# Another scratch layout for the first layer's weights, a bank pair for the first group's second scores, and a new order of the first block

## The chip, the cores and the metric

The kernel runs on one core of a Trainium2 chip. The metric is the device time of one execution in microseconds; the runs shown are three executions of the kernel before, and one more execution was profiled. Everything is in 32-bit floats at the interface.

## The reference

Local attention in chunks of 64 tokens, followed by a two-layer network with a squared ReLU:

```
q, k, v: (8, 8, 576, 64)          # batch, heads, tokens, head size
scores = q_c @ k_c^T / 8          # per head and chunk of 64 tokens
attn = exp(scores - max) / (sum + 1e-9)
x = (attn @ v_c) as (4608, 512)   # tokens x model
h = x @ w_in                      # w_in (512, 2048)
g = s * max(h, 0)^2 + b
out = g @ w_out                   # w_out (2048, 512)
```

## The kernel before

Tokens lie on 36 tiles of 128. Four tiles (512 tokens) are one column block of the first stage, which is called the layer here: two early attention groups of two tiles each, `one` and `two`, make its x, and 16 steps `up` (x times a slice of w_in, L634) and `down` (L609) run over 16 slices of the hidden dimension. The other 32 tiles are four blocks of eight tiles. In them a block of w_in or w_out is multiplied with seven products instead of eight (`p1` to `p7`, L690), with sums of quarters of the weights (units s1 to s4) and of the tokens (t1 to t4) as operands beside the plain quarters 11, 12, 22. The first of these blocks makes the sums of w_in itself (`s_add`, `s_hi`, `s_lo`); its down product is direct. The later three blocks read everything from scratch in DRAM.

Every number in a product is held as a high part and a remainder in the fast 32-bit format (`hi`, then `lo`), and a product is three matmuls: high by high, high by remainder, remainder by high.

The weights arrive as 64-bit words, in 16 pairs of 1 MB (`load0` to `load15`, L157; pair 0 in halves a and b). For each pair ScalarE runs `scale` (L172) and `tail` (L176), VectorE `shift` (L182) and `sign` (L184), GpSimd `add` (L190), ScalarE `hi` (L194) and VectorE `lo` (L198). After `lo`, SyncE stores high part and remainder to scratch: pairs of w_in by `in0` to `in7` (L204), those of w_out by `out0` to `out7` (L219), the sums by `s_keep0` to `s_keep7` (L204). The scratch of w_in is one array in the order in which the later blocks use its 56 units of 256 KB, four to a tile; so a store of a pair is cut into pieces of one or two units, and a later block loads a tile of four units with one DMA. The first block loads the exact units alone, in 14 tiles that hold one to three of them (`ring0` to `ring13`), and keeps the sums in SBUF. The pool `raw` with three buffers holds the words, and later these tiles: a load waits until the third tile before it has been used up. All these DMAs are issued by SyncE, in one queue, in order; one that waits holds up those behind it.

An early group runs in halves i = 0, 1: `scores` (L464), `peak` (L470), `sub` (L476), `exp` (L480), `sum` (L486), `normz` (L490, L491), `norm` (L495), `transposes` (L504), `copies` (L509), `values` (L516), `x_hi` (L524), `x_lo` (L528). Both halves of the scores share one PSUM tile of two banks. `up1a` and `up0a` work on the 256 tokens of `one`, `up1b` and `up0b` on those of `two`. Groups `three` to `six` make the tokens of the first block; their steps are whole (scores L368, peak L373, sub L378, sum L387, transposes L404).

Up to the end of the first block's products the order of the work is written out by hand: the string `ORDER` names the steps, and each engine takes its own in that order. `keep_busyN` is filler on TensorE, N matmuls on a tile of ones, each recorded as two instructions (L126). `s_and_b` (L1104) turns the two scalars s and b into columns with TensorE, and `sb` (L1167) copies them with VectorE. `up` of step j writes one of two PSUM banks in turn; from j = 2 on, `relu`, `square`, `g_hi` (ScalarE) and `g_lo` (VectorE, L655) read that bank, and it is free after `g_lo`. In the first block, tokens' sums are made by `xt1.add_dve` and so on (L561), and split by `.hi` (L565) and `.lo` (L570); `s_add` is four subtractions or additions (L233).

## Time and profile before

| | us |
|---|---|
| median of three runs | 786.3 |
| lowest and highest | 785.7, 787.04 |
| the profiled execution | 786.62 |
| its span from first to last instruction | 784.6 |
| TensorE busy | 771.6 |
| VectorE busy | 616.0 |
| ScalarE busy | 469.9 |
| GpSimd busy | 48.7 |

Times within the span are counted from its start. "Busy" of TensorE is the time in which a matmul is running by the profile; weight loads run beside it. A row of the timeline gives start, duration, engine, source line, operation, tiles and shapes, and in brackets how long the engine had been idle and what ended that. Durations of neighbours overlap a little, so that the distance of two starts is shorter than a duration.

### The profile page before, as it was taken

The numbers are of one execution on the slowest core, as the hardware profiler recorded it, in microseconds if no ns is written. First come the engines' busy times: TensorE is split into PE (matmuls) and PEld (weight loads), VectorE is DVE, ScalarE is ACT, GpSimd is POOL, SyncE is SP. The second block draws the span as 40 slices with busy tenths as digits, with TensorE's granted clock in tenths as the row PEclk, the third lists the DMA queues.
The fourth block names the chain that finished last, engine by engine and source line by source line (L and its number), as shares of the span: only waits on it lengthen the run. The fifth ranks groups of instructions, "written<-read, shape, count | busy, mean of one in ns | idle before, by whom it ended". The sixth has DMA issues, their size and how long they took to land.

```text
span 784.6 us, 13847 instructions
## 1 busy us (share of the span) xinstructions
PE 771.6 (98%) x5572; PEld 638.1 (81%) x5572; DVE 616.0 (79%) x892; ACT 469.9 (60%) x645; POOL 48.7 (6%) x23
## 2 busy tenths in 40 slices
PE   6899999999999999999999999999999999999997
PEld 6787887888888888888888888888888888888886
DVE  5988899998579986888899858888998723348773
ACT  3899877767653433566864635666846346575442
POOL 1453440000000000000000000000000000000000
PEclk9999999999999999999999999999999999999999
DMA  9999998778568999866566587765565778886653
GB/s 360 346 346 340 353 321 294 257 242 264 186 220 292 317 352 325 326 258 229 174 214 215 188 300 290 250 263 204 171 229 178 241 262 294 295 269 215 210 192 135
DMA packets 79988, 204.33 MB, mean 260 GB/s; under 512 B 5812, under 2 KB 39348, under 8 KB 68660
## 3 DMA queue, kind: packets, MB, share of 16 engines
q1 hardware_dynamic: 79488, 203.05, 74.4%
q8 instruction: 44, 0.72, 0.4%
q10 hardware_dynamic: 436, 0.39, 0.1%
q14 instruction: 20, 0.16, 0.1%
HBM read 159.38 MB, written 44.04 MB: 259 GB/s over the span
## 4 chain that ended last, share of the span: by engine, by line
PE 89%; ACT 4%; DVE 3%; DMA 3%; issue 0%; POOL 0%; DVEq 0%; ACTq 0%
PE ps_h L690 22%; PE ps_h L910 17%; PE ps_o L690 17%; PE ps_x L910 8%; PE ps_x L609 7%; PE ps_o L910 4%; PE ps_o L609 4%; PE ps_h L609 3%; PE ps_h L634 3%; PE ps_a L368 2%; DMA raw<-in_w_dram 1%; PE ps_x L424 1%; DMA w_out<-t 1%; ACT t L172 1%; PE ps_a L424 1%; ACT raw L176 1%
## 5 line engine op out<-in xcount | busy, mean ns | idle before, releaser
L690 PE MATMUL ps_h<-t,raw 128*128 128x512 f32 x672 | 167.3, 391 | 0.0
L690 PEld LDWEIGHTS ps_h<-t,raw 128*128 128x128 f32 x672 | 125.4, 188 | 26.5 <-ACT u L700 0.2
L910 PE MATMUL ps_h<-t,raw 128*128 128x512 f32 x576 | 142.0, 389 | 0.0
L884 DVE TENSOR_TENSOR t<-t 128x512 fp32r<-128x512 f32 (+1 forms) x120 | 105.2, 897 | 33.2 <-ACT t L882 33.2
L910 PEld LDWEIGHTS ps_h<-t,raw 128*128 128x128 f32 x576 | 108.0, 188 | 22.5
L690 PE MATMUL ps_o<-t,raw 128*128 128x512 f32 x480 | 121.8, 389 | 0.0
L709 DVE TENSOR_TENSOR t<-ps_o,u 128x512 f32<-128x512 f32 x96 | 66.0, 690 | 67.7 <-PE ps_o L690 62.4
L690 PEld LDWEIGHTS ps_o<-t,raw 128*128 128x128 f32 x480 | 90.1, 188 | 18.8
L700 ACT COPY u<-ps_h 128x512 f32<-128x512 f32 x96 | 56.0, 585 | 69.8 <-PE ps_h L690 68.9
L882 ACT CAST t<-t 128x512 fp32r<-128x512 f32 (+1 forms) x120 | 87.4, 790 | 2.8 <-PE ps_h L910 1.9
L412 DVE STREAM_TRANSPOSE pT<-p 32x256 f32<-32x256 f32 x192 | 83.7, 436 | 3.2
L910 PE MATMUL ps_x<-t,raw 128*128 128x512 f32 x288 | 73.1, 389 | 0.0
L753 ACT ACTIVATE t<-t 128x1024 f32<-128x1024 f32 x64 | 67.2, 1053 | 0.2
L910 PEld LDWEIGHTS ps_x<-t,raw 128*128 128x128 f32 x288 | 54.1, 188 | 11.3
L749 ACT ACTIVATE t<-t 128x512 f32<-128x512 f32 (+1 forms) x64 | 54.1, 846 | 10.3 <-DVE t L709 9.9
L190 POOL TENSOR_TENSOR t<-t,raw 128x1024 int32<-128x1024 int32 (+1 forms) x17 | 48.0, 2821 | 68.3 <-DVE t L184 47.8
L609 PE MATMUL ps_x<-t,raw 128*128 128x512 f32 x192 | 48.9, 390 | 0.0
L634 PE MATMUL ps_h<-x,t 128*128 128x512 f32 (+1 forms) x216 | 47.5, 371 | 1.1 <-DVE x L528 0.7
L914 ACT ACTIVATE u<-ps_h,shift,sb 128x512 f32<-128x512 f32 x18 | 13.1, 779 | 58.2 <-PE ps_h L910 58.2
L634 PEld LDWEIGHTS ps_h<-x,t 128*128 128x128 f32 x216 | 37.0, 188 | 8.5 <-DVE x L528 1.0
L609 PEld LDWEIGHTS ps_x<-t,raw 128*128 128x128 f32 x192 | 36.0, 188 | 7.5
L910 PE MATMUL ps_o<-t,raw 128*128 128x512 f32 x144 | 36.5, 389 | 0.0
(129 smaller groups left out, 1013.7 us busy)
## 6 DMA issues: line engine op xcount, KB each, us to landing
raw<-w_in SPq DMA_DIRECT2D x42, 1024.0 KB, 5.5
raw<-w_out SPq DMA_DIRECT2D x34, 1024.0 KB, 5.3
raw<-w_sum SPq DMA_DIRECT2D x24, 1024.0 KB, 5.0
raw<-in_w_dram SPq DMA_DIRECT2D x15, 1024.0 KB, 7.5
qk<-in_qkv_dram SPq DMA_DIRECT2D x15, 1024.0 KB, 8.4
w_out<-t SPq DMA_DIRECT2D x16, 512.0 KB, 6.8
w_sum<-t SPq DMA_DIRECT2D x16, 512.0 KB, 9.1
v<-in_qkv_dram SPq DMA_DIRECT2D x15, 512.0 KB, 4.7
```

What stands on the lines that cost most here:

```text
L190: nc.gpsimd.tensor_tensor(out=i, in0=i, in1=low.bitcast(I32), op=ALU.add)
L412: nc.vector.transpose(out=self.pT[k].rearrange("p i a t -> p (i a) t")[:, :, t], in_=p[t, :, k])
L609: nc.tensor.matmul(out=self.ps[m], lhsT=x, rhs=y, start=(j == 0 and i == 0), stop=(j == stop and i == 2))
L634: nc.tensor.matmul(out=self.ps[j][:, cols], lhsT=w[:, c, :], rhs=x[:, c, :], start=(c == 0 and i == 0), stop=(c == NHP - 1 and i == 2))
L690: nc.tensor.matmul(out=ps, lhsT=w[:, e, :], rhs=y[:, e, :], start=start and e + i == 0, stop=e + i == 3, skip_group_check=not start)
L700: nc.scalar.copy(out=u, in_=self.a[p])
L709: nc.vector.tensor_tensor(out=self.tile(p, h)[:, e, :], in0=ps, in1=u, op=ALU.add)
L749: nc.scalar.activation(out=t, in_=t, func=AF.Relu)
L753: nc.scalar.activation(out=t, in_=t, func=AF.Square)
L882: nc.scalar.copy(out=hi, in_=f)
L884: nc.vector.tensor_tensor(out=lo, in0=f, in1=hi.bitcast(F32), op=ALU.subtract)
L910: nc.tensor.matmul(out=self.acc[name][m], lhsT=x, rhs=y, start=new and q == 0, stop=q == 2, skip_group_check=not new)
```

## The change

- w_in's scratch becomes nine arrays: one for each of eight quarters of the exact units (`w_in[e]`, two to four units, 11 and 12 of step p beside 22 of step p - 1), and `w_in_sum` with a whole tile of four sums per step. `in` stores 11 and 12 together; `keep` is a single DMA.
- The first block loads its exact units in 8 tiles in place of 14, so the ring has 11 loads in `ORDER` in place of 17. The later blocks still take four units per tile; each load is now cut into as many DMAs as the four units have separate places (three or four).
- Group `one` takes a PSUM tile of its own for the scores of half 1, from the pool of one bank pair that the transposes use.
- `ORDER` is new. The steps are the same but for the filler: `keep_busy` 28 in place of 31, and `warm1.12`, 12 filler matmuls into the bank of `up1`. Steps `bias` and `exps` are defined and not used.

```diff
 ORDER = """
-one.load_qk0 one.load_qk1 three.load_qk load0b load0a two.load_qk0 two.load_qk1 two.load_v one.scores0 one.peak0 one.load_v s_and_b
-sb one.sub0 one.exp0 one.scores1 keep_busy7 load1 one.sum0 one.peak1 three.load_v one.normz0 one.sub1 one.norm0
-one.exp1 four.load_v tail0b one.transposes0 keep_busy3 one.sum1 one.normz1 one.copies0 load2 one.norm1 tail0a scale0a
-one.transposes1 four.load_qk shift0a scale0b two.scores0 keep_busy8 one.copies1 sign0a shift0b add0a two.peak0 two.sub0
...
-two.norm0 two.normz1 two.transposes0 keep_busy2 one.x_hi1 shift1 two.copies0 two.norm1 two.values0 sign1 two.transposes1 two.x_hi0
-one.x_lo1 two.copies1 add1 two.x_lo0 up1a scale2 tail2 two.values1 shift2 up0a hi1 sign2
-two.x_hi1 three.scores lo1 add2 two.x_lo1 in1 three.peak scale3 up1b tail3 three.sub up0b
...
-g_hi3 three.norm down0 scale4 g_lo1 hi3 shift4 relu2 g_lo3 three.transposes sign4 square2
-g_hi2 down1 load6 lo3 tail5 scale5 add4 g_lo2 in2 three.copies up4 shift5
...
+one.load_qk0 one.load_qk1 two.load_qk0 load0b load0a three.load_v one.load_v two.load_qk1 three.load_qk one.scores0 one.peak0 one.scores1
+keep_busy3 s_and_b sb one.sub0 one.peak1 one.exp0 load1 two.scores0 keep_busy13 one.sum0 one.sub1 two.load_v
+tail0b two.peak0 one.exp1 one.normz0 two.sub0 load2 tail0a one.sum1 scale0a one.norm0 two.exp0 four.load_v
+scale0b one.normz1 one.transposes0 keep_busy3 shift0a shift0b one.copies0 four.load_qk one.norm1 one.values0 sign0b one.transposes1
+one.x_hi0 sign0a two.scores1 keep_busy3 one.copies1 add0b two.sum0 one.x_lo0 two.peak1 add0a hi0b one.values1
+keep_busy6 two.sub1 one.x_hi1 lo0b load3 hi0a one.x_lo1 two.exp1 lo0a up1a two.sum1 in0
+two.normz0 tail1 up0a two.norm0 two.normz1 scale1 two.norm1 two.transposes0 shift1 two.copies0 two.transposes1 sign1
+two.values0 two.copies1 three.scores two.x_hi0 add1 tail2 two.x_lo0 two.values1 scale2 three.peak two.x_hi1 shift2
+hi1 three.sub sign2 three.exp two.x_lo1 add2 three.sum warm1.12 up1b tail3 load4 up0b
+scale3 three.normz lo1 relu1 open_o hi2 three.norm in1 up3 square1 relu0 shift3
+g_hi1 lo2 load5 square0 scale4 three.transposes sign3 out0 relu3 g_hi0 up2 shift4
+three.copies add3 square3 tail4 four.scores scale5 g_lo0 load6 g_lo1 hi3 down0 five.load_qk
+four.peak relu2 g_hi3 lo3 square2 tail5 shift5 in2 down1 sign4 g_hi2 sign5
+tail6 scale6 add4 g_lo2 g_lo3 up4 four.sub four.exp add5 load7 hi4 up5
...
+    SUMS = ("s2", "s3", "s1", "s4")
+    quarters = [[(0, "11"), (0, "12")]] + [[(p, "11"), (p, "12"), (p - 1, "22")] for p in range(1, NP)]
+    quarters[-1].append((NP - 1, "22"))
...
-    w_in = scratch.tile([P, 7 * NP // 4, 2, 4, 2 * P], F32, name="w_in")
+    w_in = [scratch.tile([P, 2, len(us), 2 * P], F32, name="w_in%d" % e) for e, us in enumerate(quarters)]
+    w_in_sum = scratch.tile([NP, P, 2, 4, 2 * P], F32, name="w_in_sum")
...
-            keep_units(units[p, "11"], i, even[:, 0:1, :])
-            keep_units(units[p, "12"], i, even[:, 1:2, :])
-            keep_units(units[p, "22"], i, odd[:, 1:2, :])
+            for name, n, source in (("11", 2, even), ("22", 1, odd[:, 1:2, :])):
+                e, u = unit_at[p, name]
+                nc.sync.dma_start(out=w_in[e][:, i, u:u + n, :], in_=source)
...
         def keep(self):
...
+            nc.sync.dma_start(out=w_in_sum[self.p], in_=self.t.bitcast(F32))
...
+                    places = [(w_in_sum[p], SUMS.index(k)) if k in SUMS else (w_in[unit_at[p, k][0]], unit_at[p, k][1])
+                              for p, k in source]
+                    u = 0
+                    while u < 4:
+                        n, (w, at) = u + 1, places[u]
+                        while n < 4 and places[n][0] is w and places[n][1] == at + n - u:
+                            n += 1
+                        nc.sync.dma_start(out=o[:, :, u:n], in_=w[:, :, at:at + n - u])
+                        u = n
...
         def scores(self, i):
-            if i == 0:
-                self.ps = self.banks(0)
+            if i == 0 or self.tb == 0:
+                self.ps[i] = self.banks(i)
+            else:
+                self.ps[i] = self.ps[0]
...
+        def warm(self, j, n):
+
+            for _ in range(n):
+                nc.tensor.matmul(out=self.ps[j][:, 2 * P:3 * P], lhsT=ones, rhs=ones, start=True, stop=True)
```

In the first block the new order of the tokens' sums and of the sums of w_in stands in the same string: before, VectorE's queue ends `... s_add0 lo15 s_add7 s_add5 s_lo0 s_lo1 g_lo15 s_add6 xt1.add_dve x22.lo xt3.add_dve xt1.lo xt2.add_dve xt3.lo seven.peak xt2.lo`; after, `... s_add7 g_lo15 g_lo14 s_lo0 lo15 s_add3 s_add5 s_add2 xt1.add_dve x22.lo xt3.add_dve xt1.lo xt2.add_dve xt3.lo xt4.add_dve xt2.lo`.

## Rows read from the trace of the kernel before

**Rows 1.** Busy time of each engine in four stretches of the span, with its count of instructions, the granted clock (1.00 is the full 2.4 GHz), the share of the DMA engines and GB/s: the opening, the layer, the first block's products, and the rest.

```profile
0.00:31.49 31.49, 23.05 (x426) 20.63 (x426) 22.45 (x42) 18.23 (x26) 7.79 (x10) 1.00 0.94 367
31.49:131.32 99.83, 99.28 (x928) 81.07 (x928) 91.78 (x108) 83.78 (x118) 40.87 (x14) 1.00 0.94 334
131.32:210.35 79.03, 78.94 (x582) 64.68 (x581) 70.16 (x114) 59.35 (x82) 0.00 (x0) 1.00 0.75 246
210.35:784.60 574.25, 570.32 (x3640) 471.74 (x3639) 431.67 (x630) 308.51 (x421) 0.00 (x0) 1.00 0.71 244
```

**Rows 2.** What TensorE waited for up to 145 us, without the early groups' own steps: us in total, times, longest.

```profile
PE ps_h L634 <- DVE t L198: 0.5, 1, 0.5
```

**Rows 3.** Timeline of TensorE in the opening: scores of `one`, `s_and_b`, and filler at two places.

```profile
4.49 1.14 PE L464 MATMUL ps_p<-t 64*64 64x64 f32 x32 [4.49 <-DMA t<-in_qkv_dram]
5.56 0.37 PE L1104 MATMUL ps_h<-ident,sb_row 1*128 1x1 f32 x2
7.17 1.14 PE L464 MATMUL ps_p<-t 64*64 64x64 f32 x32 [1.24 <-DVE t L476]
8.23 3.35 PE L126 MATMUL ps_h<-t 128*128 128x128 f32 x14
...
14.32 2.05 PE L126 MATMUL ps_h<-t 128*128 128x128 f32 x16
```

**Rows 4.** Timeline of VectorE in the opening: `sb`, `one.sub0`, and the three places with idle time over 0.5 us.

```profile
6.30 0.15 DVE L1167 COPY sb<-ps_h 128x2 f32<-128x2 f32 x1
6.42 0.69 DVE L476 TENSOR_TENSOR t<-ps_p,m 128x512 f32<-128x512 f32 x1
7.81 0.69 DVE L486 TENSOR_REDUCE z<-t 128x8 f32<-128x512 f32 x1 [0.70 <-ACT t L480]
...
14.23 0.43 DVE L182 TENSOR_SCALAR t<-t 128x512 uint32<-128x512 uint32 x1 [1.72 <-ACT t L172]
...
27.21 1.23 DVE L182 TENSOR_SCALAR t<-t 128x1024 uint32<-128x1024 uint32 x1 [0.69 <-ACT t L172]
```

**Rows 5.** The same timeline, its end: `two.x_lo1`, `three.peak`, `three.sub`.

```profile
30.75 0.68 DVE L528 TENSOR_TENSOR x<-ps_p,x 128x512 fp32r<-128x512 f32 x1
31.35 1.22 DVE L373 TENSOR_REDUCE m<-ps_a 128x16 f32<-128x1024 f32 x1
32.60 1.23 DVE L378 TENSOR_TENSOR t<-ps_a,m 128x1024 f32<-128x1024 f32 x1
```

**Rows 6.** VectorE in the layer: `shift4`, `g_lo3`, `sign4`, `lo3` and `shift5`, in this order.

```profile
41.83 0.70 DVE L182 TENSOR_SCALAR t<-t 128x1024 uint32<-128x1024 uint32 x1
42.44 0.69 DVE L655 TENSOR_TENSOR t<-ps_h,t 128x512 fp32r<-128x512 f32 x1
43.05 1.22 DVE L184 SCALAR_TENSOR_TENSOR t<-raw,t 128x1024 uint32<-128x1024 uint32 x1
44.18 1.22 DVE L198 TENSOR_TENSOR t<-t 128x1024 fp32r<-128x1024 f32 x1
...
46.61 1.65 DVE L182 TENSOR_SCALAR t<-t 128x1024 uint32<-128x1024 uint32 x1 [0.61 <-ACT t L172]
```

**Rows 7.** TensorE in the layer: `up1b` to `up2` (the first row, with its first matmul before it), the begin of `down0`, `three.transposes`, the begin of `down1`, `up4`, `four.scores`, and the place where `up8` waits.

```profile
31.49 8.47 PE L634 MATMUL ps_h<-x,t 128*128 128x256 f32 x47 [0.29 <-DVE x L528]
39.80 1.67 PE L609 MATMUL ps_x<-t 128*128 128x512 f32 x6
...
42.70 1.03 PE L404 MATMUL ps_a<-ident,t 128*128 128x128 f32 x8
43.49 1.62 PE L609 MATMUL ps_x<-t 128*128 128x512 f32 x6
...
46.30 2.88 PE L634 MATMUL ps_h<-x,t 128*128 128x512 f32 x12
49.12 1.16 PE L368 MATMUL ps_a<-qk 64*64 64x64 f32 x64
...
67.52 2.55 PE L634 MATMUL ps_h<-x,t 128*128 128x512 f32 x10 [0.48 <-DVE t L198]
```

**Rows 8.** SyncE's queue: the six stores of a pair of w_in, with the time from the first issue to the end of the last.

```profile
93.20 7.89 SPq L204 DMA_DIRECT2D w_in<-t  x6
```

**Rows 9.** Begin of the first block: four subtractions of an `s_add` (VectorE), `xt2.lo` (VectorE), and products among which the first is the one that reads it (TensorE).

```profile
104.52 1.55 DVE L233 TENSOR_TENSOR t<-t 128x256 f32<-128x256 f32 x4
...
135.25 1.22 DVE L570 TENSOR_TENSOR t<-t 128x1024 fp32r<-128x1024 f32 x1
...
137.15 5.71 PE L690 MATMUL ps_h<-t,x 128*128 128x512 f32 x24
```

**Rows 10.** DMA issues of the whole program by kind: count, KB each, median us from issue to landing.

```profile
raw<-w_in SPq DMA_DIRECT2D x42, 1024.0 KB, 5.5
raw<-w_out SPq DMA_DIRECT2D x34, 1024.0 KB, 5.3
...
raw<-w_in SPq DMA_DIRECT2D x12, 256.0 KB, 3.8
```

**Rows 11.** Begin of the second block: the issue of two tiles by SyncE, the landing of the first of them (the one DMA of 317 to 318 us), and the products of TensorE just ahead of those that use it.

```profile
317.14 5.76 SPq L330 DMA_DIRECT2D raw<-w_in  x2
raw<-w_in SPq DMA_DIRECT2D x1, 1024.0 KB, 11.3
328.58 1.66 PE L690 MATMUL ps_h<-t,raw 128*128 128x512 f32 x6
```

194 lines of the change are left out of this document (100 added, 94 removed).

## The prediction

> **What bounds the kernel now.** I first read the busy time of each engine by stage, cut at four places: the first matmul of the layer's first unbroken stretch (31.49 us), the first product of the first block (131.32) and the first matmul of its direct down product (210.35). TensorE is busy 99.28 of 99.83 us in the layer, 78.94 of 79.03 in the first block and 570.32 of 574.25 behind it; only in the first 31.49 us is it busy a mere 23.05, and part of that is filler [rows 1]. So the change can give at most the opening, some tenths in the layer, and the end, which it doesn't touch. It can take much more, since every wait of TensorE behind 31.49 us goes whole into the time.
>
> Next, TensorE's waits up to 145 us: 4.5 us for the first q and k [rows 3], some short ones inside the early groups, and 0.5 us for a weight remainder (`lo`, L198) [rows 2]. Third, the queues of the opening. VectorE is the one that matters: from the first subtraction (`one.sub0`, 6.42) to the start of `two.x_lo1` (30.75), which releases `up1b` at 31.49, are 24.3 us, with idle time of 0.70, 1.72 and 0.69 us [rows 4, 5]. Work is thus 21.2 us of it. The time goes with VectorE's order here, not with TensorE or the transfers.
>
> **Opening, beginning.** The second scores get a bank pair of their own, so they no longer wait for `one.sub0`, which had cost TensorE the gap from 5.93 to 7.17 [rows 3]. But `s_and_b` is moved behind `one.scores1` and `keep_busy3`, and on VectorE the copy `sb`, which needs it, still stands ahead of `one.sub0`. TensorE: 4.49, scores 1.14 twice with an overlap of 0.1, then `keep_busy3` as six instructions (3.35/14 = 0.239 each, 1.43), then 0.37: the end is at 8.4. `sb` (0.15) had run at 6.30 and `one.sub0` at 6.42; now `one.sub0` starts near 8.5. That adds 2.1 us at the head of VectorE's queue, and behind it stand all of its work of the opening. Filler took 2.05/16 = 0.128 later on, with a granted clock of 1.00 (the 2.4 GHz level) for the whole stretch [rows 1, 3]; by that price the delay would be 1.4. I take 0.239, the row nearest in time.
>
> **Opening, loads.** The order of the loads changes, their bytes don't. `three.qk`, third before, is now ninth: 5.2 MB at 367 GB/s put it at about 15 us [rows 1], and `three.scores` take it near 26, behind `two.values0`. The q and k of the second scores come second as before. Cost 0; if `three.qk` came 11 us later than that, `three.scores` would hold TensorE's queue.
>
> **Opening, rest.** Between `one.sub0` and `two.x_lo1` the new order has the same VectorE work, less `lo1` (1.13 from start to start, as [rows 6] shows for this form), with `three.peak` and `three.sub` (1.25 [rows 5], and 1.13 as its like) put ahead. So 21.2 + 1.25 + 1.13 - 1.13 = 22.4 us, from 8.5: 30.9 if VectorE never waits. It will wait: the first transposes now stand behind `keep_busy13`, 26 instructions of 0.239 (6.2 us, to about 15.4) or of 0.128 (3.3), while their input is ready near 13.8; `one.x_lo0` then lacks up to 0.8, `two.x_lo0` and `shift2` some 0.5 and 0.4 for ScalarE's results. Bounds are 0 and 1.7; I take 1.05. `two.x_lo1` then starts at 31.95 against 30.75: **+1.2 us** (bounds +0.15 and +1.9). `warm1.12` (24 instructions, 3.1 us) stands behind `two.values1`, which I place at 28.3, and ends near 31.4, so VectorE's later result covers it; without that cover it would cost up to 3.1.
>
> **Layer.** From `up1b` to the end of `up2` are 8.3 us [rows 7]. New in between: `three.transposes` (0.8), and behind `up2`, ahead of `down0`, `four.scores` (1.09). With `up1b` at 32.7: `four.scores` run from 41.8 to 42.9, `down0` and `down1` (2.8 each) to 48.4, then `up4`. That needs the PSUM bank of `up3`, free after `g_lo3`. Before, `g_lo3` was done at 43.13 and `up4` came at 46.30, a slack of 3.2 [rows 6, 7]. Now `four.peak` stands ahead on VectorE and waits there for `four.scores`, to 42.9; queued behind it are `lo3`, `shift5`, `sign4`, `sign5`, `g_lo2` and `g_lo3`. From 42.9: 1.13 + 1.14 + 0.65 + 1.14 + 1.14 + 0.6 + 0.69 = 49.4. So TensorE waits 1.0 at `up4`; with a late `hi3` (0.6) or the shift at its long duration (1.65 against 0.70) up to 2.6 [rows 6]. I take **+1.6**; below 0 is excluded, since it is a wait, and 0 is possible if the order of ScalarE brings `scale5` and `hi3` early. Old `up8` lost 0.5 at 67.52 waiting for weights; with TensorE 2.8 us later that goes: **-0.5** [rows 7]. All other VectorE and ScalarE steps of the layer are shuffled without being added; they lie beside TensorE's 99.83 us and cost nothing while the slack holds.
>
> **Scratch, stores.** In the layer six stores of 128 KB per pair become four, and seven of a sums tile become one of 1 MB. The six from 93.20 held SyncE's queue for 7.89 us, ahead of a weight load [rows 8]. Weights come earlier by some us; the only wait this removes is the 0.5 counted above. Nothing more: up to 145 us TensorE waits for a load itself only at the very start [rows 3].
>
> **First block.** The joining order is new, its work the same. The one tight place: product `p6` needs `xt2.lo`, which before started at 135.25 and was done 0.7 us ahead of the products of 137.15 [rows 9]. Ahead of `xt2.lo` come one `s_add` (1.55) and `xt4` (1.13) more and `s_lo1` and `seven.peak` (1.13 each) less: +0.4, inside the slack. But VectorE gains waits in the layer too. Bounds 0 and 1.6 (the slack gone and a whole `s_add` late); I take **+0.2**. The eight ring loads hold three units in place of 1.7: each frees a buffer later, but a unit is still loaded two buffers ahead.
>
> **Later blocks.** Each of 42 loads of 1 MB becomes three or four issues with pieces of 1 KB rows. Loads of whole rows land in 5.5 us, those from w_out, partly in such pieces, in 5.3, those of 256 KB in 3.8 [rows 10]. A tile is taken up in 5.4 us with two more waiting: hidden. The thinnest cover is at a block's start: the load issued at 317.14 landed in 11.3, at 328.4, and its first user comes near 329.9 [rows 11]. I take 0, bounds 0 and 2 us for each of three starts. The end of the program is unchanged.
>
> **Sum.** 1.2 + 1.6 - 0.5 + 0.2 = +2.5 us. The profiled execution took 786.62 (span 784.6 and 2.0 around it); the median of the runs is 786.3. Forecast: 786.3 + 2.5 = 788.8. With all bounds but those of the later blocks: 0.15 + 0 - 0.5 = -0.35 up to 1.9 + 2.6 - 0.5 + 1.6 = +5.6, so 786.0 to 791.9.
>
> **Rivals.** (a) *No difference.* VectorE catches up in the layer, where it was busy 91.78 of 99.83 [rows 1]: `up4` isn't kept waiting, and only 1.2 - 0.5 = +0.7 remains, 787.0. It is decided by whether `g_lo3` ends before `down1`. For it: the slack of 3.2 before. Against it: six steps behind `four.peak`.
> (b) *Faster.* `s_and_b` is done early enough that `one.sub0` starts near 6.5. Then 6.5 + 22.4 = 28.9 for `two.x_lo1` without waits, 1.85 earlier; the 0.5 in the layer goes, and the earlier weights leave no wait at `up4`: -2.35 in all, 784.0. It decides at a start of `one.sub0` under 7.3. For it: the scores no longer wait for a bank. Against it: `sb` in VectorE's queue, and the price of the filler.
> (c) *Slower by the pieces.* SyncE's issue time at a backlog was 7.89/6 = 1.3 us for one small transfer [rows 8]; a tile of four would be issued in 5.3 in place of 0.33, land 5 us later, and take more than the 1.5 us of cover at a block's start: 2 us at each of three starts, 788.8 + 6 = 794.8. Against it: the 256 KB loads, which landed in 3.8. The Trainium skill (DMA: Bandwidth & Descriptors, section Bandwidth) advises batches of at least 1 MiB, which speaks against just this edit; by the fixed 2.0 us and the 436 KB per us of its section on the anatomy of one DMA, four pieces in series would be an estimated 10.4 us against 4.4 for one. The trace speaks for overlap, with 3.8 us for 256 KB and 5.5 for 1 MB, though no run here shows a tile cut so.
>
> **Chances.** Forecast 0.50, (a) 0.28, (b) 0.15, (c) 0.07. A measurement of this kernel tells about 0.2% (1.6 us) from no change. A fifth of the forecast's own spread lies under 787.9. So faster 0.15, same 0.28 + 0.10 = 0.38, slower 0.40 + 0.07 = 0.47. The range reaches half a us below (b), for its own spread, and up to the end of the known bounds, and leaves (c) out: 783.5 to 792.0; the forecast's own is 786.0 to 791.9.
>
> **What would show it.** `one.sub0` at 8.5; `two.x_lo1` at 32 and `up1b` at 32.7; a TensorE wait of 1 to 2 us near 48 at L634 with L655 as its releaser; none at 67; the first product of the block at 133 to 134; no TensorE waits in the later blocks. I am wrong if `one.sub0` starts before 7.3, if `up1b` starts before 31.5, or if TensorE waits at L690 for transfers.

## The result and the profile after

The changed kernel takes 794.65 us (median of four runs, 793.8 to 795.15) against 786.67 for the kernel before on the same chip (785.7 to 787.34): a ratio of 1.0092, 95% interval 1.0074 to 1.011. It is 8.0 us slower where 2.5 had been forecast. The profiled execution has a span of 793.2, 8.6 more than before. The same stretches as in [rows 1], cut at the same places (`up1b`, first product, first matmul of the direct down product), with the busy times of TensorE, its weight loads, VectorE, ScalarE and GpSimd, the granted clock, the share of the DMA engines and GB/s:

```profile
0.00:32.81 32.81, 24.23 (x444) 21.58 (x444) 22.94 (x43) 18.41 (x26) 6.52 (x10) 1.00 0.95 370
32.81:136.65 103.84, 99.55 (x928) 81.08 (x928) 93.11 (x109) 82.70 (x117) 36.62 (x14) 1.00 0.90 324
136.65:220.25 83.60, 82.68 (x600) 67.79 (x598) 72.21 (x113) 61.07 (x84) 0.00 (x0) 1.00 0.62 228
220.25:793.20 572.95, 567.69 (x3623) 468.54 (x3621) 430.69 (x629) 307.83 (x420) 0.00 (x0) 1.00 0.73 243
```

The opening is 1.32 us longer than before. The layer is 4.01 longer (103.84 against 99.83) although TensorE is busy for only 0.27 us more in it: the rest is waiting. Counted from block to block instead of by this cut, the first block is 1.06 longer and the rest 2.2. All that TensorE waited for between 32 and 145 us (total, times, longest), where there had been one wait of 0.5 [rows 2]:

```profile
PE ps_h L658 <- ACT ps_h L675: 2.2, 1, 2.2
PE ps_h L658 <- DVE t L684: 1.5, 1, 1.5
PE ps_h L658 <- DVE x L552: 1.3, 1, 1.3
PE ps_o L724 <- ACT o L637: 0.9, 1, 0.9
PE ps_a L369 <- ACT pT L418: 0.4, 1, 0.4
PE ps_a L425 <- ACT pT L418: 0.2, 1, 0.2
```

The first two stand in the layer, at `up6` and `up4`; the third lies ahead of it, in front of `up1b`; the fourth is in the first block. The last two, 0.4 at 105.76 and 0.2 near 128, are small attention products that wait for ScalarE.

In the opening the forecast's steps can be read one by one. TensorE (timeline), the answer to [rows 3]: `s_and_b` ends at 8.97 where 8.4 was expected, `keep_busy13` takes 3.17 us for its 26 instructions, and the first transposes then wait 1.42 for VectorE.

```profile
8.60 0.37 PE L1138 MATMUL ps_h<-ident,sb_row 1*128 1x1 f32 x2
...
9.97 3.17 PE L125 MATMUL ps_h<-t 128*128 128x128 f32 x26
14.55 0.63 PE L528 MATMUL ps_a<-ident,t 128*128 128x128 f32 x4 [1.42 <-DVE z L493]
```

VectorE, the answer to [rows 4, 5]: `sb` after 2.42 us of idleness, `one.sub0` at 9.09, `two.x_lo1` at 32.07, which lets `up1b` go at 32.81.

```profile
9.01 0.16 DVE L1203 COPY sb<-ps_h 128x2 f32<-128x2 f32 x1 [2.42 <-PE ps_h L1138]
9.09 0.68 DVE L479 TENSOR_TENSOR t<-ps_p,m 128x512 f32<-128x512 f32 x1
...
32.07 0.68 DVE L552 TENSOR_TENSOR x<-ps_p,x 128x512 fp32r<-128x512 f32 x1
```

The two large waits of the layer, on TensorE, where [rows 7] had none: `up4` and `up6`.

```profile
50.63 5.74 PE L658 MATMUL ps_h<-x,t 128*128 128x512 f32 x24 [1.49 <-DVE t L684]
...
62.61 2.97 PE L658 MATMUL ps_h<-x,t 128*128 128x512 f32 x12 [2.21 <-ACT ps_h L675]
```

VectorE ahead of `up4`, the answer to [rows 6]: `shift4`, `g_lo0` and `g_lo1`, `four.peak`, `lo3`, `shift5`, `sign4` and `sign5`, `g_lo2` and `g_lo3`. TensorE goes on at 50.63, when the first of the last two is done (the two of the last row take 0.68 each, so that one ends at 50.57). Ahead of `lo3` VectorE sat idle for 0.56: `lo3` waited for ScalarE's `hi3` and not for `four.peak`, which had ended at 45.31.

```profile
40.05 0.69 DVE L188 TENSOR_SCALAR t<-t 128x1024 uint32<-128x1024 uint32 x1
40.65 3.52 DVE L684 TENSOR_TENSOR t<-u,t 128x512 fp32r<-128x512 f32 x2
44.10 1.21 DVE L374 TENSOR_REDUCE m<-ps_a 128x16 f32<-128x1024 f32 x1
45.87 1.23 DVE L204 TENSOR_TENSOR t<-t 128x1024 fp32r<-128x1024 f32 x1 [0.56 <-ACT t L200]
47.01 0.69 DVE L188 TENSOR_SCALAR t<-t 128x1024 uint32<-128x1024 uint32 x1
47.61 2.35 DVE L190 SCALAR_TENSOR_TENSOR t<-raw,t 128x1024 uint32<-128x1024 uint32 x2
49.89 1.28 DVE L684 TENSOR_TENSOR t<-ps_h,t 128x512 fp32r<-128x512 f32 x2
```

And the chain of what released what, up to `up6`, as the profile gives it (start, us, what). It runs through two transfers: `load5`, issued behind the stores of `in1`, and `load7`, issued at 52.31, when `add4` has given up its buffer. `scale7` waits for it on ScalarE (60.00), and more steps of ScalarE stand behind it, `square5` (62.10) the last of them.

```profile
37.05 6.71 DMA raw<-in_w_dram
...
43.78 1.12 ACT t L178
44.90 0.95 ACT t L200
...
47.70 2.28 DVE t L190 x2
...
50.01 2.28 POOL t L196
...
52.31 7.61 DMA raw<-in_w_dram
...
60.00 1.14 ACT t L178
...
62.10 0.51 ACT ps_h L675
62.61 2.97 PE ps_h L658 x12
```

The last link is only the step that ended last by the profile. What `up6` needs is the bank that `g_lo4` gives up, and `g_lo4`, on VectorE, stands behind `shift7`, which needs `scale7`:

```profile
61.17 0.69 DVE L188 TENSOR_SCALAR t<-t 128x1024 uint32<-128x1024 uint32 x1 [2.52 <-ACT t L178]
61.78 0.68 DVE L684 TENSOR_TENSOR t<-ps_h,t 128x512 fp32r<-128x512 f32 x1
```

`g_lo4` ends at 62.46, 0.15 before `up6`. In all the runs below whose `up6` waits, it starts 0.05 to 0.15 us behind that end; in e13 `square5` had by then been done for 2.2 us.

At the begin of the first block [rows 9] the second product waits 0.92 us: ScalarE copies a bank out (`st2`, L637, 138.46) only behind a cast that had to wait for VectorE's sum.

```profile
137.50 1.05 ACT L589 CAST t<-t 128x1024 fp32r<-128x1024 f32 x1 [1.22 <-DVE t L585]
138.46 0.58 ACT L637 COPY o<-ps_o 128x512 f32<-128x512 f32 x1
```

```profile
139.09 1.67 PE L724 MATMUL ps_o<-t,raw 128*128 128x512 f32 x6 [0.92 <-ACT o L637]
```

The cut loads, the answer to [rows 10], by kind: in the later blocks and the ring 96 loads of sums, 66 of exact units by the place that they come from. A piece lands 5.2 and 4.8 us after its own issue, where a whole tile of 1 MB took 5.5. The pieces of a tile are issued one behind another, about 0.6 us each (two in 1.18 at 336.66), so a tile of four is whole some 2 us later than one piece.

```profile
raw<-w_in_sum SPq DMA_DIRECT2D x96, 256.0 KB, 5.2
...
raw<-w_in SPq DMA_DIRECT2D x66, 256.0 KB, 4.8
```

No wait for a transfer stands at the start of the second block [rows 11]. Behind 145 us TensorE's side has one, 0.33 us at 710.19, where a weight load waits for a tile of `w_out`.

### The profile page after: what moved, and what is told of

Read it like the earlier page. It is cut to its first block, busy times and chain, and to the rows that moved or that the text cites. A ratio compares the mean times of both kernels' runs of the same rounds, so it can differ in the third digit from the quotient of the medians.

```text
span 793.2 us, 13983 instructions
## 1 busy us (share of the span) xinstructions
PE 774.2 (98%) x5590; PEld 639.0 (81%) x5590; DVE 619.0 (78%) x892; ACT 470.0 (59%) x645; POOL 43.1 (5%) x23
## 4 chain that ended last, share of the span: by engine, by line
PE 87%; DVE 5%; DMA 4%; ACT 2%; issue 1%; POOL 0%; SPq 0%; DVEq 0%; ACTq 0%; POOLq 0%
PE ps_h L724 22%; PE ps_o L724 17%; PE ps_h L944 17%; PE ps_x L944 8%; PE ps_x L633 6%; PE ps_o L944 4%; PE ps_o L633 3%; DMA raw<-in_w_dram 3%; PE ps_h L633 3%; PE ps_h L658 3%; PE ps_a L369 2%; PE ps_x L425 1%; DVE t L190 1%; DVE t L204 1%; DVE t L230 1%
## 5 line engine op out<-in xcount | busy, mean ns | idle before, releaser
L734 ACT COPY u<-ps_h 128x512 f32<-128x512 f32 x96 | 56.2, 586 | 70.4 <-PE ps_h L724 69.3
L196 POOL TENSOR_TENSOR t<-t,raw 128x1024 int32<-128x1024 int32 (+1 forms) x17 | 42.4, 2503 | 81.4 <-DVE t L190 46.3
```

The source lines that it names most:

```text
L196: nc.gpsimd.tensor_tensor(out=i, in0=i, in1=low.bitcast(I32), op=ALU.add)
L734: nc.scalar.copy(out=u, in_=self.a[p])
```

## The experiments

All were run beside the kernel before on the same chip. "Up1b" and "first product" are starts of TensorE in the profiled run; the layer is the distance between them. Waits and other readings of a profile stand in the text.

| run | median | before | ratio [95%] | up1b | first product | layer |
|---|---|---|---|---|---|---|
| before | 786.67 | | | 31.49 | 131.32 | 99.83 |
| changed | 794.65 | 786.67 | 1.0092 [1.0074, 1.011] | 32.81 | 136.65 | 103.84 |
| e1 | 786.41 | 786.83 | 0.9987 [0.9974, 1.0] | 30.69 | 130.27 | 99.58 |
| e2 | 804.29 | 786.83 | 1.0207 [1.018, 1.0234] | 32.68 | 137.61 | 104.93 |
| e3 | 792.43 | 786.83 | 1.006 [1.0037, 1.0083] | 32.45 | 135.94 | 103.49 |
| e4 | 794.69 | 786.83 | 1.0094 [1.0065, 1.0123] | 33.29 | 134.84 | 101.55 |
| e5 | 790.94 | 787.9 | 1.0043 [1.0028, 1.0058] | 32.47 | 134.61 | 102.14 |
| e6 | 793.58 | 787.9 | 1.0072 [1.0055, 1.0089] | 31.74 | 140.06 | 108.32 |
| e7 | 792.45 | 787.9 | 1.0056 [1.0038, 1.0074] | 31.42 | 136.47 | 105.05 |
| e8 | 793.9 | 787.9 | 1.008 [1.0065, 1.0095] | 33.19 | 135.85 | 102.66 |
| e9 | 791.67 | 786.48 | 1.0067 [1.0047, 1.0087] | 32.36 | 133.77 | 101.41 |
| e10 | 793.75 | 786.48 | 1.0099 [1.0084, 1.0115] | 32.76 | 135.72 | 102.96 |
| e11 | 795.09 | 786.48 | 1.011 [1.0095, 1.0126] | 32.60 | 137.97 | 105.37 |
| e12 | 804.17 | 786.48 | 1.0219 [1.0193, 1.0245] | 32.68 | 133.16 | 100.48 |
| e13 | 794.57 | 787.39 | 1.0083 [1.0055, 1.0111] | 32.71 | 137.74 | 105.03 |
| e14 | 794.41 | 787.39 | 1.0081 [1.0053, 1.011] | 32.63 | 134.24 | 101.61 |
| e15 | 796.53 | 787.39 | 1.0111 [1.0079, 1.0142] | 32.37 | 137.62 | 105.25 |
| e16 | 786.6 | 787.39 | 0.9983 [0.9966, 1.0] | 31.47 | 131.25 | 99.78 |
| e17 | 794.09 | 787.68 | 1.0087 [1.0066, 1.0109] | 32.49 | 135.28 | 102.79 |
| e18 | 791.46 | 787.68 | 1.0051 [1.0033, 1.0069] | 32.71 | 136.45 | 103.74 |

### Which part costs: scratch or order (e1, e2)

e1 has the new scratch, its cut loads and eight ring tiles, with the order of before and the shared banks of the scores; each ring load stands right behind the last user of the tile three before it.

```diff
-ORDER of the changed kernel, its ring0 to ring10 as in the change
+ORDER of the kernel before, with ring0 to ring10 in place of ring0 to ring16
-            if i == 0 or self.tb == 0:
+            if i == 0:
```

> The kernel before with the new scratch and its eight ring loads alone: old order of the steps (ring loads placed behind the last user of the tile that they replace), old bank for the second scores. Theory A (the order causes most): the opening and the layer are as before, up1b at 31.5 us and the first block's first product at 131 to 132 us; only the later blocks lose, most of it in the second block (162.9 us before, 164.8 after the change): +1.5 to +3 us in all. Theory B (the scratch causes most, because stores of other sizes reach the weight loads through SyncE's queue): the first block's first product at 134 us or later and +5 us or more in all.

0.9987 with an interval that reaches 1.0: not slower. The layer takes 99.58, the second block 162.95 us as before. The scratch, its stores and the cut loads cost nothing that can be measured, and the 1.5 to 3 us that theory A gave them are missed as well as theory B's 5.

e2 is the reverse: the old scratch and its 14 ring tiles, with the new order, the bank pair and `warm1.12`.

```diff
-ORDER of the kernel before
+ORDER of the changed kernel, with ring0 to ring16, each behind the last user of the tile three before
+            if i == 0 or self.tb == 0:
+                self.ps[i] = self.banks(i)
```

> The kernel before with the new order, bank pair and warm matmuls alone; scratch, its stores and the loads of the later blocks as before (ring loads placed behind the last user of the tile that they replace, and the first matmuls of the direct down product, d0, moved behind the load that they need). Theory A: up1b at 32.8 us, first block's first product at 135.5 to 137, the second block's length as before (162.9 us): +5 to +6.5 us. Theory B: +2.5 us at most, the opening's 1.3 and little else.

Slower by 2.1%, with the first product at 137.61: the order alone brings the whole loss and more, which neither theory had (+5 to +6.5 and +2.5 at most). Of the more, 6.17 us stand at one place, the first `down` weights behind the longer ring, which my placing of the ring loads has to answer for; so e2 prices nothing exactly. The cause lies in the order.

### Which half of the order (e3 to e6)

The order is cut at `two.x_lo1`: up to it from one kernel, what is left in the order of the other. All four have the new scratch; e3 and e5 the new opening and the own bank pair, e4 and e6 the new layer and first block; e5 and e4 with `warm1.12`, e3 and e6 without.

```diff
# e3
 ORDER: the changed kernel's up to two.x_lo1, then
-three.sum warm1.12 up1b tail3 load4 up0b scale3 three.normz lo1 relu1 ...
+what is left, in the order of the kernel before
```

> The changed kernel with the new order only up to two.x_lo1; behind it all steps stand in the order of the kernel before. Theory A, with the layer's order as the culprit: up1b at 32.8, the layer's length back to 100 us (first product at 132.5 to 133.5), and with the scratch's 2 to 2.7 us in the later blocks +3.5 to +4.5 us in all. If instead the late opening itself makes the layer's waits (all that follows is 1.3 us late and the weights with it), the layer stays near 103 us or longer and the time at +7.

```diff
# e4
-ORDER of the changed kernel up to two.x_lo1
+ORDER of the kernel before up to two.x_lo1, then
 what is left, in the order of the changed kernel, warm1.12 among it
```

> The other half: the order of before up to two.x_lo1 (and its shared bank), the new order behind it, new scratch. Theory A: up1b at 31.5, but the layer 102.5 to 104 us long, first product at 134.5 to 135.5, +6 to +7 us in all. If the late opening makes the layer's waits: layer near 100 us, +3 to +4 us in all.

```diff
# e5, against e3
 ... two.x_lo1
+warm1.12
 ... up1b
```

> As the run with the new opening and the old order behind it, with the change's 12 filler matmuls put back ahead of up1b; in that run they were missing, TensorE idled 2.7 us and its granted clock was 0.83 from 20 to 40 us. Theory A1 (the layer was slow there by the clock, not by its order): clock 1.00, up1b at 32.5, layer back to 99.6 to 100.5 us, first product at 132 to 133, +1.5 to +2.5 us against the kernel before. Theory A2 (the late opening drags the weights): layer stays at 102 us or more, +4 us or more.

```diff
# e6, against e4
 ... two.x_lo1 add2 three.sum
-warm1.12
 up1b ...
```

> Old order up to two.x_lo1 (shared bank), new order behind it, without the 12 filler matmuls, which in the run with them stood between two.x_lo1 and up1b and held up1b to 33.3 us. up1b then at 30.7. If the new order of the layer costs by itself: layer 102 us or more and the first product at 132.5 to 134, +3 to +5 us. If it costs only in company with the late opening: first product at 130.5 to 131.5, 0 to +2 us.

Both halves cost. The new opening alone costs 0.43% (e5), of which 1.0 us is the later `up1b` and 2.3 come in the old layer behind it. The new layer costs 0.7 to 0.9% even behind the old opening (e4, where `up1b` stands behind the filler, and e6, where a wait of 2.96 and a lower clock follow in its absence). In e4 GpSimd's `add0` to `add2` run as early as before (`add2` at 29.6 against 29.8), yet `add3` starts at 40.7 against 35.8: the new layer order puts `three.sum`, `three.normz`, `three.norm` and `lo2` ahead of `sign3` on VectorE. That is the delay of the weights, and it doesn't hang on the opening.

e3 and e5 show what the filler is for. Between the two stands only `warm1.12`. TensorE at `up1b`, first e3, then e5:

```profile
32.45 10.94 PE L658 MATMUL ps_h<-x,t 128*128 128x256 f32 x47 [2.73 <-DVE x L552]
```

```profile
32.47 8.49 PE L658 MATMUL ps_h<-x,t 128*128 128x256 f32 x47 [1.29 <-DVE x L552]
```

`up1b` starts at the same time, but behind 2.73 us without a matmul the 47 take 2.45 us longer, and the granted clock of 20 to 40 us is 0.83 in e3 against 1.00 in e5. The ratios differ by 0.0017, inside their intervals, so what the filler is worth in the whole time isn't shown.

### The opening's 1.3 us, and the stores (e7, e8)

```diff
# e7
-one.peak0 one.scores1 keep_busy3 s_and_b sb one.sub0
+one.peak0 s_and_b sb one.scores1 keep_busy3 one.sub0
```

> The changed kernel with s_and_b right behind the first scores and sb right behind one.peak0, as before; all else as changed. By the step of the prediction that sb holds one.sub0 for 2 us: one.sub0 at 6.7 in place of 9.1, two.x_lo1 0.5 to 1.9 us earlier (VectorE gets new waits for the weights), up1b at 31 to 32.3. Weights of the layer come earlier too: -1 to -3 us against the changed kernel (791.5 to 793.5). If another queue sets two.x_lo1, no change.

`up1b` comes 1.39 earlier, at 31.42, and the first product at 136.47 all the same: waits of 1.32 at `up4` and 2.48 at `up6`. Behind the 2.48 the 12 matmuls of `up6` take 4.39 us in place of 2.97, at a granted clock of 0.83 from 60 to 70: that alone is the 1.4 us gained ahead of the layer. So the opening's price, taken away, isn't seen at the first product of this execution. The median, 792.45, is inside the expected 791.5 to 793.5 all the same and 2.2 us under the changed kernel's, with intervals that just touch; the profiled execution was the slowest of its runs.

```diff
# e8
-in1 up3 square1 relu0 shift3 g_hi1 lo2 load5 square0
+up3 square1 relu0 shift3 g_hi1 lo2 load5 in1 square0
```

> The changed kernel with the stores in1 moved behind load5 in SyncE's queue; in the changed kernel load5 (issued at 37.05) stood behind these four stores, which waited for lo1 until 36.1. Theory: that is the head of the chain load5, sign4, add4, load7, scale7, up6, so load5 comes near 33, load7 2 to 3 us earlier, the wait of 2.2 us at up6 falls under 1 us and that of 1.5 at up4 under 1: -1.5 to -3 us against the changed kernel. Rival: load7 waits for add4, and that for VectorE's order, not for load5: under 0.7 us.

`load5` goes out about 1.9 us earlier, and the wait at `up4` falls to 0.83; at `up6` 2.11 stay. The stores ahead of a load hold a part only, and the time, 793.9, is the rival's (under 0.7 us).

### The waits at up4 and up6 (e9 to e12)

```diff
# e9
-four.peak relu2 g_hi3 lo3 square2 tail5 shift5 ... g_lo2 g_lo3 up4
+relu2 g_hi3 lo3 square2 tail5 shift5 ... g_lo2 g_lo3 four.peak up4
```

> The changed kernel with one step moved on VectorE: four.peak behind g_lo3 in place of ahead of lo3. Theory P (the prediction's step for the wait at up4: four.peak stands ahead of lo3, shift5, sign4, sign5, g_lo2 and g_lo3): lo3 starts 1.1 us earlier and TensorE's wait of 1.49 us at up4 falls to 0.4 or less. Theory L (the weights' chain: load5 lands late, scale5 waits for it on ScalarE and holds up hi3, which lo3 needs): lo3 still starts at 45.8 or 45.9, the wait at up4 stays at 1.3 to 1.6, and the time stays within 0.5 us of the changed kernel's 794.6.

```diff
# e10
-four.scores scale5 g_lo0 load6 g_lo1 hi3 down0
+four.scores g_lo0 load6 g_lo1 hi3 scale5 down0
```

> The changed kernel with scale5 moved behind hi3 on ScalarE, so that hi3 no longer stands behind a step that waits for load5. Theory L: hi3 starts when add3 is done, near 43.0 in place of 44.80; lo3 then waits for four.peak alone and starts near 45.2 in place of 45.87, so the wait at up4 falls from 1.49 to about 0.9. Theory P: four.peak alone holds lo3, so hi3 may come earlier but the wait at up4 stays at 1.4 to 1.5. The wait of 2.21 us at up6 is untouched by either.

```diff
# e11: both
-four.scores scale5 g_lo0 load6 g_lo1 hi3 down0 five.load_qk four.peak relu2 ... g_lo3 up4
+four.scores g_lo0 load6 g_lo1 hi3 scale5 down0 five.load_qk relu2 ... g_lo3 four.peak up4
```

> Both moves, scale5 behind hi3 on ScalarE and four.peak behind g_lo3 on VectorE. Theory L: lo3 starts near 44.1 (hi3 from 43.0 to 44.05), g_lo3 ends near 49, and up4 waits 0.3 us or not at all; sign4 and so add4 and load7 come about 1.7 us earlier, so up6's wait falls from 2.21 to about 0.5 to 1.0. The first block starts 2.5 to 3 us earlier than in the changed kernel (133.6 to 134.2), and the time is 791.5 to 792.5. If the waits only move to a later step, the first block still starts at 136 or later, and the time is 794.

At `up4` e9 leaves 0.93, e10 0.84, e11 0.77. In e9 `lo3` still waits 1.14 us for `hi3`, which stands behind `scale5` and so behind `load5`; it starts earlier, at 44.85, since `load5` landed in 6.1 us in place of 6.7. So e9's 0.56 isn't the price of `four.peak`. In e10, where `hi3` no longer stands behind `scale5`, `lo3` starts right behind `four.peak`, at 45.19: the late `hi3` is worth 0.65, and `four.peak` is the next in line. In e11, with both out of the way, `lo3` comes at 43.92, but then `shift5` waits 0.79 for `scale5`, that is for a `load5` that took 7.9 us. At `up6` e9 waits 0.86, e10 2.44, e11 3.34. e9's better `up6` goes with a `load7` that landed in 5.8 us, against 7.7 and 8.0 in e10 and e11; e11's prediction failed outright, and its waits moved to a later step.

```diff
# e12
-    big = ... bufs=33      raw = ... bufs=3      op = ... bufs=4
+    big = ... bufs=32      raw = ... bufs=4      op = ... bufs=2
```

> The changed kernel with four buffers for the words and later tiles in place of three, paid for with one slot of the large pool (32 in place of 33) and two output buffers (2 in place of 4). Theory: load7 is issued at 52.31 only because its buffer was held until add4 ended; with a fourth buffer it is issued by 46 at the latest, right behind load6 and the stores of in2, lands by 54, and the wait of 2.21 us at up6 is gone (at most 0.3 left). The wait of 1.49 at up4 hangs on load5, which stands behind the stores of in1 in SyncE's queue and not on a buffer, so it stays at 1.0 to 1.5. First block at 134.5 to 135, time 792 to 793. Rival: the DMA engines are full, more loads in flight land no earlier, and the wait at up6 stays at 1.5 or more.

The order is the changed kernel's, word for word. SyncE's timeline and TensorE's:

```profile
47.49 0.39 SPq L163 DMA_DIRECT2D raw<-in_w_dram  x1
```

```profile
50.10 5.75 PE L658 MATMUL ps_h<-x,t 128*128 128x512 f32 x24 [1.07 <-DVE t L684]
...
59.73 2.88 PE L658 MATMUL ps_h<-x,t 128*128 128x512 f32 x12
```

`load7` goes out at 47.49 in place of 52.31, `up6` doesn't wait, and the layer takes 100.48 in place of 103.84. So with the fourth buffer the 2.21 us are gone: with three, a load stands behind an `add`, and the new order runs the adds late. The late issue is only a part of the cause; the transfer's length is the other. In e4 `load7` went out as late against TensorE (53.26, 1.66 us behind the start of `up4`; 52.31 and 1.68 in the changed kernel) but landed in 5.2 us in place of 7.6, and `up6` doesn't wait there either. The kernel as a whole is 2.2% slower, against 792 to 793 expected: it has waits that the changed kernel hasn't, one of 3.65 at 314.72 for L637 and three of 3.7 in all for L734. Whether the two output buffers or the slot that paid for the fourth buffer are missed there wasn't tried apart.

### The weights first, and what came in the way (e13, e17, e18, e14)

```diff
# e13
-in1 up3 ... lo2 load5 square0        scale5 g_lo0 load6 g_lo1 hi3
+up3 ... lo2 load5 in1 square0        g_lo0 load6 g_lo1 hi3 scale5
-four.peak relu2 g_hi3 lo3 square2 tail5 shift5 in2 down1 sign4 g_hi2 sign5 ... g_lo2 g_lo3 up4
+relu2 g_hi3 lo3 sign4 square2 tail5 shift5 in2 down1 g_hi2 sign5 ... g_lo2 g_lo3 four.peak up4
-down15 eight.load_qk xt3.add_dve xt1.lo xt3.hi p1.0 st2
+down15 st2 eight.load_qk xt3.add_dve xt1.lo xt3.hi p1.0
```

> The changed kernel with five steps moved, all for the weights: the stores of in1 behind load5 (SyncE), scale5 behind hi3 (ScalarE), four.peak behind g_lo3 and sign4 ahead of shift5 (VectorE), st2 ahead of xt3.hi (ScalarE, begin of the first block). Theory (the order of the queues sets the weights' chain): load5 is issued near 35, hi3 starts near 43, sign4 near 45.2 in place of 47.6, add4 ends near 49 in place of 52.3, load7 is issued then and lands by 57. The wait at up4 falls from 1.49 to 0.5 or less, the one at up6 from 2.21 to 0.3 or less, the 0.92 at p2.0 to 0.3 or less. The opening is unchanged (up1b at 32.8). First block at 133.3, time 789.5 to 791. Rival (a later opening costs this anyway): the waits return at up8 or later steps, the first block starts at 135.5 or later, time 793 or more.

`sign4` came at 45.20 and `load7` went out at 49.34, both as expected, and the wait at `up4` grew to 1.99. VectorE (`shift5`, `sign5`, the two `g_lo`), then GpSimd's `add4`:

```profile
46.34 0.69 DVE L188 TENSOR_SCALAR t<-t 128x1024 uint32<-128x1024 uint32 x1
47.06 3.33 DVE L190 SCALAR_TENSOR_TENSOR t<-raw,t 128x1024 uint32<-128x1024 uint32 x1
50.32 1.28 DVE L684 TENSOR_TENSOR t<-ps_h,t 128x512 fp32r<-128x512 f32 x2
```

```profile
46.55 2.76 POOL L196 TENSOR_TENSOR t<-t,raw 128x1024 int32<-128x1024 int32 x1 [3.61 <-ACT ps_h L675]
```

`sign5` takes 3.33 where it takes 1.22 elsewhere. It ends at 50.39: `add4`'s end, 49.31, and 1.08 more, about its own time. It stood still until GpSimd was done. `load7` then took 9.6 us, and behind the 1.99 us without a matmul 24 of them took 7.37 in place of 5.74, at a granted clock of 0.83 from 50 to 60.

```diff
# e17, against e13
-shift5 in2 down1 g_hi2 sign5 ... g_lo2 g_lo3 four.peak up4
+shift5 four.peak in2 down1 g_hi2 ... g_lo2 g_lo3 sign5 up4
```

> As the run with the weights' steps first, but on VectorE four.peak, g_lo2 and g_lo3 stand ahead of sign5, so that the work of VectorE while add4 runs reads its first operand from PSUM. Theory (an instruction of VectorE that works on SBUF alone waits until GpSimd's add has ended, one that reads PSUM does not): four.peak keeps its 1.21 and starts near 47.1 although add4 runs from 46.5 to 49.3; sign5 takes 1.22 in place of 3.33; the two g_lo come near 49, and the wait at up4 falls from 1.99 to 0.5 or less. At up6 shift7 still meets add6, and the wait of about 1.75 stays. Rival (what lengthens VectorE's steps is the traffic of the transfers, whatever they read): one of the steps from 46.5 to 49.3 still takes 2 us or more, and the wait at up4 stays at 1.5 or more.

VectorE's timeline and GpSimd's `add4` (46.33 to 49.10):

```profile
46.72 1.22 DVE L374 TENSOR_REDUCE m<-ps_a 128x16 f32<-128x1024 f32 x1
47.88 1.29 DVE L684 TENSOR_TENSOR t<-ps_h,t 128x512 fp32r<-128x512 f32 x2
49.09 1.22 DVE L190 SCALAR_TENSOR_TENSOR t<-raw,t 128x1024 uint32<-128x1024 uint32 x1
```

```profile
46.33 2.77 POOL L196 TENSOR_TENSOR t<-t,raw 128x1024 int32<-128x1024 int32 x1 [3.61 <-ACT ps_h L675]
```

Three steps that read PSUM (`ps_a`, `ps_h`) run beside `add4` at their usual length, `sign5` is 1.22 again, and `up4` doesn't wait at all. That it is the meeting with GpSimd and not the traffic is shown: the DMA engines were at 0.98 to 0.99 from 40 to 50 us in both. But `up6` is reached earlier and now waits 3.33, where about 1.75 had been expected; `load7` took 9.0 us.

```diff
# e18, against e17
-scale7 down2 sign6 in3 three.x_out shift7 square5 add6 g_lo4 tail7 up6
+down2 sign6 in3 three.x_out square5 scale7 add6 g_lo4 shift7 tail7 up6
```

> The kernel of the run before it, and in addition g_lo4 ahead of shift7 (VectorE) and square5 ahead of scale7 (ScalarE), so that what frees the banks for up6 and up7 stands behind no step that waits for load7. Theory: the wait at up6 falls from about 1.75 to 0.4 or less, wherever load7 lands; with up4's also gone the first block starts 3 to 3.5 us earlier than in the changed kernel, at 133.0 to 133.8. The begin of the block keeps 0.7 to 1.0. Time 790 to 791.5. Rival (the weights themselves are late): a wait of 1 us or more moves to up7 or up8, the first block starts at 135 or later, time 793 or more.

```profile
59.05 3.02 PE L658 MATMUL ps_h<-x,t 128*128 128x512 f32 x12 [0.40 <-DVE t L684]
...
69.51 0.73 PE L658 MATMUL ps_h<-x,t 128*128 128x512 f32 x2 [1.12 <-ACT t L200]
70.77 3.76 PE L658 MATMUL ps_h<-x,t 128*128 128x512 f32 x10 [0.52 <-DVE t L204]
```

The wait at `up6` is down to 0.40 as expected, and the rival is right about the rest: 1.64 us come back at `up8`, this time for the weights themselves (`hi7`, `lo7`), and the 12 matmuls there take 4.5 us in place of 2.9 at a clock of 0.83. The first product of the profiled execution is at 136.45, hardly earlier than in the changed kernel. The median, 791.46, is 3.2 us under the changed kernel's, inside the 790 to 791.5 that the theory gave, with intervals that don't meet; that gain isn't seen in the profile's first product. Taking a wait away in front of a late chain shows the next one.

```diff
# e14: e9, and
-down15 eight.load_qk xt3.add_dve xt1.lo xt3.hi p1.0 st2
+down15 st2 eight.load_qk xt3.add_dve xt1.lo xt3.hi p1.0
```

> The changed kernel with four.peak behind g_lo3 (VectorE), as in the run before with that move alone (791.67 us), and st2 ahead of xt3.hi on ScalarE. Theory: the 0.92 us at p2.0 comes from st2, which frees a bank and stands behind xt3.hi; it falls to 0.3 or less, and the time is 0.5 to 0.9 us lower than without this second move, 790.8 to 791.2. Rival: the block's begin is set by VectorE's sums; a wait of 0.5 to 0.9 stays at one of the next products, and the time stays at 791.7.

The 0.92 at the second product is gone, and 0.72 stand a few products later for VectorE's `lo` (L594): the rival was right. `up4` and `up6` wait 0.92 and 0.86 as in e9. The time, 794.41, has a wide interval and tells nothing against e9's.

### The filler, and a beginning of its own (e15, e16)

```diff
# e15
-three.sum warm1.12 up1b
+three.sum up1b
```

> The changed kernel without warm1.12, the 12 filler matmuls ahead of up1b. Theory W: the gap of TensorE before up1b grows from 1.29 to about 4 us, the granted clock falls under 1.00 in the stretch from 30 to 45, and the 35 matmuls recorded with up1b in one group take 6.5 to 8 us in place of 5.96; the waits at up4 and up6 take up part of that, so the time is 795.2 to 797. Rival: the filler covers nothing, the clock stays at 1.00, the time stays at 794.2 to 795.

```profile
32.37 7.27 PE L658 MATMUL ps_h<-x,t 128*128 128x256 f32 x35 [2.74 <-DVE x L552]
```

As theory W has it, with a shorter gap than expected (2.74): 7.27 in place of 5.96 us, a granted clock of 0.83 from 30 to 40, 796.53 us. The wait at `up4` falls to 0.29 in exchange. Against the changed kernel the two intervals overlap, so the loss in the whole time isn't shown.

```diff
# e16, against e1
-one.load_qk1 three.load_qk ... one.load_v s_and_b sb one.sub0 one.exp0 one.scores1
+one.load_qk1 ... one.load_v three.load_qk s_and_b sb one.scores1 one.sub0 one.peak1 one.exp0
-tail0a scale0a one.transposes1 ... shift0a
+one.exp1 scale0a ... one.normz1 shift0a
+            if i == 0 or self.tb == 0:
```

> The new scratch with the order of the kernel before, as in the run of that alone (786.41 us), and a beginning of its own: a bank pair for the second scores, which stand right behind s_and_b and sb, so that one.sub0 stays where it was; three.load_qk three loads later; scale0a and shift0a earlier. Theory: VectorE's idle time of 0.70 and 1.72 in the opening goes in part, up1b starts 0.5 to 2 us earlier than in the run of the scratch alone (30.69), at 28.7 to 30.2, the layer keeps its 99.6, and the time is 784 to 786. Rival (the weights set the layer's pace): up1b starts earlier, but the first block still starts at 130.3 or later, and the time stays at 786.0 to 786.8.

`up1b` didn't come earlier than in e1 but 0.8 later (31.47). The time is that of the rival, 786.6, a ratio of 0.9983 with an interval up to 1.0. The bank pair can be had for nothing; a gain from it isn't shown, and neither e1 nor e16 is a kernel that clearly beats the one before.

## Why the prediction was wrong

**Opening: right.** +1.2 was forecast for `up1b`, +1.32 came. `one.sub0` was expected at 8.5 and came at 9.09, since TensorE's start, the filler (0.275 for each of six) and `sb` were all a little late; `keep_busy13` fell to the lower price, 3.17, and cost the transposes nothing: they waited 1.42 for VectorE. The size owes something to luck: `one.sub0` was 0.6 late and `two.x_lo1` only 0.12 (32.07 against 31.95), since VectorE lost about 0.5 less in waits between the two than had been allowed. The cover that `warm1.12` was said to have (+0) holds: `up1b` waited for VectorE in either case.

**"Ends near 31.4, so VectorE's later result covers it": half of it.** The filler costs nothing, but its absence would: e3 and e15 show a lower clock and 1.3 to 2.5 us longer matmuls. The prediction gave it no worth.

**up4: the size right by luck, the way in part.** +1.6 was forecast, 1.49 came. `four.peak` was the reason given, but in the changed kernel `lo3` waited for `hi3`, not for `four.peak`: `load5` landed at 43.76, `scale5` and then `hi3` followed on ScalarE, and `lo3` started at 45.87. The prediction had the late `hi3` at 0.6; `lo3` came 1.84 later than before. Against that it counted both of the last two `g_lo`, where `up4` goes on behind the first (0.6 too much), and TensorE reached `up4` 0.74 later than it had reckoned, at 49.14. These errors cancel. `four.peak` is the next in line: with `hi3` out of the way (e10) it sets `lo3`. And VectorE was late ahead of both: `four.peak` started at 44.10, not at 42.9. Some 0.6 of that is `four.scores`, which ended at 43.46; the other 0.6 is one `g_lo`, which took 2.92 us at 40.65 while GpSimd's `add3` ran:

```profile
40.26 2.76 POOL L196 TENSOR_TENSOR t<-t,raw 128x1024 int32<-128x1024 int32 x1 [5.53 <-DVE t L190]
```

`add3` ended at 43.02; a `g_lo`'s 0.6 more make 43.6, where this one ended (40.65 and 2.92 are 43.57). The prediction reckoned with 0.69 for each such step and took the 1.65 of `shift5` [rows 6] for a spread of durations. In the kernel before, GpSimd's `add4` was the reason there too:

```profile
44.39 3.31 POOL L190 TENSOR_TENSOR t<-t,raw 128x1024 int32<-128x1024 int32 x1 [5.27 <-DMA raw<-in_w_dram]
```

It ends at 47.70, and `shift5` of [rows 6], 46.61 and 1.65 long, ends at 48.26, its own 0.6 behind.

**The step that failed: "All other VectorE and ScalarE steps of the layer are shuffled without being added; they lie beside TensorE's 99.83 us and cost nothing while the slack holds", and with it "Weights come earlier by some us".** The slack didn't hold. Against before, `add2` starts 2.45 us later (32.28 against 29.83), `add3` 4.4, `add4` 4.6 (48.97 against 44.39), `load7` 4.6 (52.31 against 47.73). With three buffers a late `add` is a late load. The late load, which also took 7.61 us to land, comes back through `scale7` on ScalarE and `shift7` on VectorE to `g_lo4`, which gives up the bank: 2.21 us at `up6`, at a place that the prediction had priced at nothing. e12 shows it, with the same order and a fourth buffer; e4 shows that a transfer of 5.2 us would have hidden as late an issue. The 0.39 and 0.20 at two later places weren't traced to a cause; 0.20 stands in e12 too, and 0.4 in e16 with the old layer. I had priced the stores' queue, and not asked when each load gets its buffer.

**-0.5 at the old up8: right.** No wait stands there.

**First block: too small.** +0.2 with a bound of 1.6 was forecast for VectorE's sums, 1.06 came, mostly the 0.92 of a bank copy on ScalarE, which the prediction hadn't looked at. By e14 VectorE would have cost 0.72 anyway.

**Later blocks: 0 for the pieces is right (e1).** Rival (c) is out: e1 has the pieces, loses nothing, and they land in about 5 us each, beside one another; its 794.8 is near the measured time by chance. The advice of the Trainium skill that was cited for it, batches of at least 1 MiB (DMA: Bandwidth & Descriptors, section Bandwidth), speaks against the pieces. e1, which has them, lost nothing (0.9987). The profiled run still lost 1.86 us in its second block (164.80 against 162.94), 1.33 of it waits at small attention products (L369) that the profile gives no releaser for, and 0.35 further on, about the 0.33 of the wait for `w_out`. e9 and e18 have the same order and the same cut loads there and take 162.97 and 162.95. But such waits stand in 13 of the 18 profiles with the new scratch, e17's with the same 1.3 us, and in neither of the two with the old. So whether they belong to the change, and why some executions have them, stays open; e1 and e16, with the new scratch, have none and are no slower.

**The sum**, from the profiles: 1.32 + 4.01 + 1.06 + 1.86 + 0.35 = 8.6, against 1.2 + 1.1 + 0.2 + 0. The range ended at 792.0, since the layer's upper bound took in `up4` alone. What stays open is a version of the new order that keeps the weights as early as before; e18, the fastest with the new layer, is still 0.51% slower than the kernel before.

## What to carry to other kernels

When an order written by hand is changed, follow the transfers' ring round once: when is a buffer given up, by which engine, and what stands behind the step that waits for the load; here 4.6 us of delay in a step of GpSimd, with a transfer of 7.6 us behind it, came back as 2.2 us on TensorE, two engines further. An engine with nine tenths of its time busy has no free order: moving a step ahead of another moves all that hang on the other. And a wait removed in front of a late chain can come back further down the chain (e11, e17, a part of it in e18), or as a lower clock (e7).
